# Attention scores as float32 products on two half-height tiles of TensorE, in a bucketed-attention kernel with a two-layer network behind it

## The chip, the cores and the metric

The kernel runs as one program on one core of a Trainium2 chip. What is compared is the device time of one execution in microseconds (us). The kernel before took 938.75 us, the median of three runs (938.37 to 939.9).

## The reference

```python
def _attn_ref(q, k, v, proj):                 # q, k, v: (4, 8, 768, 64) float32; proj: (64, 6)
    scale = 1.0 / np.sqrt(D)
    q_bits = (np.einsum('bhsd,dk->bhsk', q, proj) > 0).astype(np.int64)
    k_bits = (np.einsum('bhsd,dk->bhsk', k, proj) > 0).astype(np.int64)
    q_bucket = np.sum(q_bits * 2 ** np.arange(6), axis=-1)
    k_bucket = np.sum(k_bits * 2 ** np.arange(6), axis=-1)
    mask = q_bucket[:, :, :, None] == k_bucket[:, :, None, :]
    scores = np.where(mask, scale * np.matmul(q, k.transpose(0, 1, 3, 2)), -1000000000.0)
    attn = np.exp(scores - np.max(scores, axis=-1, keepdims=True))
    attn = attn / (np.sum(attn, axis=-1, keepdims=True) + 1e-09)
    return np.matmul(attn, v).astype(np.float32)

x = np.ascontiguousarray(attn_out.transpose(0, 2, 1, 3)).reshape(B * S, H * D)   # (3072, 512)
h = np.maximum(x @ w_in, 0.0)                 # w_in: (512, 2048), float64 in memory
return (h * h @ w_out).astype(np.float32)     # w_out: (2048, 512), float64 in memory
```

A query sees only the keys whose six sign bits are the same as its own. All results are wanted to nearly the precision of float32, so the kernel works with float32 products or with numbers split into a leading and a remaining part.

## The kernel before, in words

Work comes in **units** of 128 queries of one head: 4 batches x 8 heads x 6 = 192 units. `unit` (line 569) issues a unit's scores on TensorE (`pS`, 128 queries x two halves of 384 keys), the row maximum on VectorE (`nmx`), the exponential with its sum on ScalarE (`e`), the reciprocal of the sum (`rv`), the weights as a leading and a remaining float16 part (`hl`, ScalarE and VectorE) and a transposing DMA to `aT`, which brings the keys to the partitions.

`prep` (line 495) makes a head's operands. The kernel has two ways for the scores:

- The first 8 heads that are visited (`PLAIN`, line 47) are **plain**: one 128-row stack holds 64 rows of q and 64 rows of bucket indicators for one operand, k and its indicators for the other, in float32. A unit is then two float32 products of 384 columns. The profile shows each float32 product as two records, one for each of its two passes over the columns.
- The other 24 heads use the type float32r, in which a product is one pass. k and q are split into a leading and a remaining part, stacked in 128 rows as `A` and `Q`, `L` and `M`, and a unit is four products of 384 columns (`pS<-A,Q` twice, `pS<-L,M` twice).

The bucket's part comes from the **projections** `pd` (signs of 24 rows: both halves of k and of q), which ScalarE turns to `bits`, and from two products `pc` of `bits` with a table of signs, which VectorE writes into the stacks. A plain head has two float32 products `pd`, another head six float32r ones.

`av` (line 601) multiplies the weights with the values `VV` for 384 queries of one head: six products on the whole array and then, with `pair` (line 594), three times two products side by side, which go to the left and the right 64 columns of the array. For the first eight heads `av_both` (line 618) lays both halves of the queries side by side in 18 such pairs. The sum `x32` is then split into `xx` by `moe`.

`moe` (line 633) is the two-layer network for 384 tokens, eight times: 16 x 12 products `pm` of 384 columns and 16 x 9 products `po` of 512 columns, all in float32r.

Nothing is issued in the order in which it is written. `Program.order` (line 206) makes a list schedule from data, buffers and rough costs (`cost`, line 169), and `emit` (line 356) issues each engine's queue in that order; so nearly every instruction has line 382 or 379 in the profile. `PACE` ties the network's products to the units' numbers, so that they fill TensorE while attention goes on. `emit` also puts products for nothing (`idle`, line 375) where the schedule leaves TensorE idle before the first `pm`.

Of the kernel before, what the change touches and what calls it, by code (L numbers as in the profile page):

```python
# [23 lines left out]
P = 128  # L24
# [44 lines left out]
class View:  # L69
    """A part of a tile that is made when the first instruction that uses it is issued."""  # L70
# [37 lines left out]
class Program:  # L108
    """Instructions as written, and the order in which the engines' queues take them: a list
    schedule over their data, buffers and rough costs. Tile adds every wait."""  # L110
# [58 lines left out]
    def cost(key, name, args, kw):  # L169
        """(queue's time, time until the result can be used)"""  # L170
        size = lambda x: int(np.prod(x.shape[1:]))
        if name == "matmuls":
            return 188, 188
# [3 lines left out]
        if key == "pe":  # L177
            t = max(107, size(args[2]) * (4 if args[2].dtype == F32 else 1) / 2.4 + 3)
            return t, t
# [15 lines left out]
    @staticmethod  # L195
    def port(key, name, args, kw):
        """Whether the instruction takes the SBUF port that VectorE and GpSimd share."""
# [8 lines left out]
    def order(self):  # L206
# [28 lines left out]
    def backward(self):  # L235
        """For each instruction how late it could start, by a schedule from the end, latest first."""
# [42 lines left out]
    def forward(self, prio, near):  # L279
# [8 lines left out]
        out, dma, dge, held = [], 0.0, 0.0, 0.0  # L288
# [11 lines left out]
        while True:  # L300
# [94 lines left out]
def lsh_attention_moe(ctx: ExitStack, tc, kq, v, proj2, w_in, w_out, consts, out):  # L395
# [36 lines left out]
    # constants: the masks' offsets and bounds, the scales, the signs' threshold; the signs of a bucket's bits,  # L432
    # for k's and q's buckets of each half; the unit matrix
    cst = sb([P, 4], F32, "cst")
    sp.dma_start(cst, consts[:, 0:4])
    pj = sb([P, 5 * NB], F32, "pj")
    sp.dma_start(pj, proj2)
    pjh = sb([P, 5 * NB], F32R, "pjh")
    pjl = sb([P, 5 * NB], F32R, "pjl")
    move(pjh, pj)  # L440
    left(pjl, pj, 1.0, pjh.bitcast(F32))
    sgn_f = sb([4 * NB, 2 * P], F32, "sgn_f", tag="xt")
    sp.dma_start(sgn_f, consts[0 : 4 * NB, 4 : 4 + 2 * P])
    sgn = sb([4 * NB, 2 * P], BF16, "sgn")
    dve.tensor_copy(sgn, sgn_f)
    unit_f = sb([P, P], F32, "unit_f", tag="xt")
# [19 lines left out]
    def split(src, hi, lo):  # L466
        # all but each number's last two bytes: four, whose first 19 bits end the float32, and the first two
# [23 lines left out]
    # ---- operands of one head: stacks of 128 rows for the products  # L491
    f32 = lambda x: x.bitcast(F32)
    xss = {}

    def prep(b, h, plain):
        r0 = pr.rank
        dt = F32 if plain else F32R
        tags = ("A", "Q") if plain and h % 2 else ("L", "M")
        R = sb([P, S], F32, tags[0] if plain else "R", 2 if plain else 1)
        M = sb([P, S], dt, tags[1], 2)  # L500
        send(R, kq[b, h])
        if plain:
            # k, all rows but its bucket's | q, its bucket's row
            Rq = sb([D, S], F32, "Rq")
            send(Rq, kq[b, h, U])
            products, stacks = ((pj, R),), ((M, R),)
        else:
            # kh kh | qh ql, and kl, all rows but its bucket's | qh, its bucket's row
            A = sb([P, S], F32R, "A", 2)
            L = sb([P, S], F32R, "L", 2)  # L510
            Q = sb([P, S], F32R, "Q", 2)
            move(A, R, cst[:, 2:3])
            left(L, R, cst[:, 2:3], f32(A))
            products, stacks = ((pjh, A), (pjl, A), (pjh, L)), ((Q, A), (M, L))
        # sides of the projections: NB rows each for k's first and second half and for q's
        pd = ps([P, 512], F32, "pd", tag="misc")[0 : 4 * NB, 0:HS]
        todo = [(p[:, (1 - half) * NB : (5 - half) * NB], x[:, half * HS : (half + 1) * HS]) for p, x in products for half in range(2)]
        for n, (p, x) in enumerate(todo):
            pe.matmul(pd, p, x, start=n == 0, stop=n == len(todo) - 1)
        bits = sb([4 * NB, HS], BF16, "bits")  # L520
        act.activation(bits, pd, AF.Sign, scale=2.0**60, bias=cst[0 : 4 * NB, 3:4])
        pr.rank = r0 + STACKS
        if not plain:
            move(Q[T], f32(A[U]), 1.0, MV)
            move(Q[U], f32(L[U]), 1.0, MV)
            move(A[U], f32(A[T]), 1.0, MV)
        for half in range(2):
            w = slice(half * HS, (half + 1) * HS)
            pc = ps([P, 512], F32, "pc", tag="misc")[:, 0:HS]
            pe.matmul(pc, sgn[:, half * P : (half + 1) * P], bits, start=True, stop=True)  # L530
            dve.tensor_scalar(M[:, w], pc, cst[:, 0:1], cst[:, 1:2], ALU.subtract, ALU.max)
        if plain:
            move(R[U], M[T], 1.0, MV)
            move(M[T], Rq, SC)
        else:
            move(L[U], f32(M[T]), 1.0, MV)
            move(M[T], f32(Q[T]), 1.0, MV)
        return stacks
# [29 lines left out]
    # ---- 128 queries: scores, softmax, and its weights with keys on the partitions  # L568
    def unit(st, half, i, aT):
        stacks = st[0]  # L570
        c0 = half * HS + i * P
# [22 lines left out]
    def pair(pA, w, x, stop):  # L594
        """The products of two chunks of keys side by side, in the array's left and right columns."""
        pr.add((pe, "matmuls", [((pA[m, 0:HS], w[:, n], x[:, n]), {"start": False, "stop": stop}) for n, m in enumerate((T, U))], {}))
# [201 lines left out]
```

## Time and profile before

| | |
|---|---|
| runs | 938.75 us median (938.37 to 939.9) |
| span of the profiled execution | 936.9 us; what the runs' median has beyond it is 1.85 us |
| TensorE (PE) busy | 918.7 us, 98% of the span, 4865 products |
| VectorE (DVE) busy | 646.1 us, 69% |
| ScalarE (ACT) busy | 758.6 us, 81% |
| first product of the network (`pm`) | 144.7 us |
| last product | ends at 931.7 us |
| granted TensorE clock | 0.999 |

The profile gives the span of one execution from its first to its last instruction; the execution's own time is that span, and the runs' times have a little around it. Records of TensorE overlap, because the next product starts while the last one drains. So the mean duration of a product in the groups is not its price. Its price is the distance from its start to the start of the next group, which the timeline gives; there, a row is a run of like instructions with its start in us, its length, and the number of records. An operation's shape is given as the part of the array that it uses (128\*128, 128\*64: 64 of its columns, 24\*128: 24 of its rows) and the columns that stream through.

### The profile page before, as it was taken

What the parts mean: (1) busy time and instruction counts of PE and PEld (TensorE: products, weight loads), DVE (VectorE), ACT (ScalarE), POOL (GpSimd) and SP (SyncE); (2) the same over time, 40 slices, a digit from 0 to 9 for tenths busy, and PEclk for the clock granted to TensorE, in tenths of its full rate; (3) what the DMA queues carried; (4) which work ended last, traced back from release to release, by engine and by line L of the source; (5) the groups of instructions that cost most, each with busy time, mean ns of one, the idle gap of its engine ahead of it and who ended that gap; (6) DMA issues with size and microseconds to landing.
All of it is one profiled execution on the core that took longest, in us unless ns stands there. A gap on an engine that the chain in (4) does not pass through costs nothing.

```text
span 936.9 us, 14136 instructions
## 1 busy us (share of the span) xinstructions
PE 918.7 (98%) x4865; PEld 699.0 (75%) x4865; DVE 646.1 (69%) x1178; ACT 758.6 (81%) x1332; POOL 74.3 (8%) x142
## 2 busy tenths in 40 slices
PE   8999899999999999999999999999999999999997
PEld 4444447888777777777787778777786888998896
DVE  6999899999888878878788777877777322211111
ACT  5999899999999999999999998978998544433433
POOL 0210121123200000100000000000100000000000
PEclk9999999999999999999999999999999999999999
DMA  8999999999999889998899989989849853633433
GB/s 246 225 225 208 205 237 270 270 280 284 223 270 227 191 185 220 219 198 196 200 222 214 199 201 195 222 181 208 189 121 218 190 146 113 174 125 113 160 122 102
DMA packets 335643, 187.16 MB, mean 200 GB/s; under 512 B 305212, under 2 KB 305364, under 8 KB 335572
## 3 DMA queue, kind: packets, MB, share of 16 engines
q1 hardware_dynamic: 335572, 186.26, 84.2%
q8 instruction: 39, 0.64, 0.3%
q14 instruction: 32, 0.26, 0.1%
HBM read 96.04 MB, written 14.68 MB: 118 GB/s over the span
## 4 chain that ended last, share of the span: by engine, by line
PE 82%; ACT 1%; DVE 0%; issue 0%; ACTq 0%; POOL 0%; POOLq 0%
PE po L382 30%; PE pm L382 28%; PE pS L382 11%; PE pA L382 5%; PE pA L379 4%; PE pd L382 3%; PE pc L382 1%; ACT g L382 0%; ACT e L382 0%; ACT hl L382 0%; DVE f L382 0%; ACT o L382 0%; DVE nmx L382 0%; PE pt L382 0%; ACT A L382 0%
## 5 line engine op out<-in xcount | busy, mean ns | idle before, releaser
L382 PE MATMUL po<-wo,g 128*128 128x512 f32 x1152 | 365.4, 406 | 0.2 <-DVE g L382 0.2
L382 PE MATMUL pm<-xx,win 128*128 128x384 f32 x1536 | 344.2, 341 | 0.3 <-DVE g L382 0.2
L382 PEld LDWEIGHTS pm<-xx,win 128*128 128x128 f32 x1536 | 273.6, 188 | 17.2 <-issue 4.7
L382 PEld LDWEIGHTS po<-wo,g 128*128 128x128 f32 x1152 | 211.8, 188 | 49.1 <-issue 14.8
L382 DVE TENSOR_REDUCE nmx<-pS 128x1 f32<-128x768 f32 x192 | 183.1, 954 | 69.4 <-PE pS L382 68.3
L382 DVE SCALAR_TENSOR_TENSOR hl<-e,rv,hl 128x768 f16<-128x768 f32 x192 | 196.4, 1025 | 17.3 <-ACT hl L382 16.6
L382 ACT ACTIVATE e<-pS,nmx 128x768 f32<-128x768 f32 x192 | 171.8, 895 | 19.9 <-DVE nmx L382 12.6
L382 ACT ACTIVATE hl<-e,rv 128x768 f16<-128x768 f32 x191 | 176.1, 927 | 8.2 <-DMA aT<-hl 4.3
L382 DVE SCALAR_TENSOR_TENSOR g<-g,g 128x384 fp32r<-128x384 f32 x116 | 64.9, 560 | 134.8 <-ACT g L382 134.0
L382 ACT ACTIVATE g<-pm 128x384 f32<-128x384 f32 x126 | 61.3, 487 | 118.2 <-PE pm L382 117.1
L382 ACT ACTIVATE g<-g 128x384 f32<-128x384 f32 (+1 forms) x236 | 122.6, 520 | 4.2 <-DVE g L382 0.3
L382 PE MATMUL pS<-A,Q 128*128 128x384 f32 x384 | 116.9, 392 | 3.1 <-ACT e L382 2.6
L382 PE MATMUL pS<-L,M 128*128 128x384 f32 x384 | 112.3, 381 | 3.4 <-ACT e L382 2.5
L382 PEld LDWEIGHTS pS<-A,Q 128*128 128x128 f32 x384 | 68.1, 188 | 25.7 <-ACT e L382 7.2
L382 POOL TENSOR_SCALAR rv<-sm 128x1 f32<-128x1 f32 x107 | 41.5, 388 | 577.3 <-ACT e L382 573.3
L382 PEld LDWEIGHTS pS<-L,M 128*128 128x128 f32 x384 | 68.7, 188 | 16.6 <-ACT e L382 5.7
L379 PE MATMUL pA<-aT,VV 128*64 128x384 f16 x576 | 67.7, 335 | 0.5 <-DMA aT<-hl 0.5
L382 PE MATMUL pA<-aT,VV 128*128 128x384 f16 x288 | 65.8, 330 | 1.1 <-DMA aT<-hl 0.9
L379 PEld LDWEIGHTS <-VV 128*64 128x64 f16 x576 | 27.2, 108 | 40.5 <-issue 34.2
L382 PEld LDWEIGHTS <-VV 128*128 128x128 f16 x288 | 23.3, 97 | 30.4 <-issue 20.6
L382 DVE TENSOR_SCALAR M<-pc,cst 128x384 fp32r<-128x384 f32 (+1 forms) x56 | 37.6, 672 | 7.3 <-PE pc L382 6.9
L382 ACT ACTIVATION_READ_ACCUMULATOR e<-pS,nmx 128x1 f32 x192 | 36.9, 192 | 0.0
(79 smaller groups left out, 663.1 us busy)
## 6 DMA issues: line engine op xcount, KB each, us to landing
wo<-wo_d SPq DMA_DIRECT2D x112, 512.0 KB, 3.9
R<-kq SPq DMA_DIRECT2D x24, 384.0 KB, 4.4
wo_d<-wo SPq DMA_DIRECT2D x16, 512.0 KB, 4.4
raw<-w_in SPq DMA_DIRECT2D x16, 511.8 KB, 5.0
raw<-w_out SPq DMA_DIRECT2D x16, 511.8 KB, 4.7
RV<-vp SPq DMA_DIRECT2D x16, 384.0 KB, 3.9
out<-o SPq DMA_DIRECT2D x24, 256.0 KB, 3.8
aT<-hl SPq DMA_TRANSPOSE x192, 4.5
```

What stands on the lines that cost most here:

```text
L379: ins = q.engine.matmul(*map(real, args), **kw).ins
L382: ins = getattr(q.engine, o.name)(*map(real, o.args), **{k: real(x) for k, x in o.kw.items()}).ins
```

## The change

All heads now take one way. `prep` loads k as `K`, with the first 384 keys in the upper 64 partitions and the other 384 in the lower 64, and q as `Q`, the same 64 rows in both halves of the partitions. The scores of a unit are two float32 products with 64 rows each: the first runs on the array's upper 64 rows, the second on its lower 64. The bucket's indicators are no longer rows of the same stack but matrices `kM` and `qM` in bfloat16, whose two products of 64 rows are added to the scores in PSUM. No leading and remaining parts of k and q are made any more. The projections are three float32 products for each head, of 32 columns each, at column positions 0, 32 and 64 of the array; three `pc` products with 32 rows each follow.

The values of two heads of a pair are multiplied side by side: 18 times two products of 64 columns for 384 queries of both heads. The sum is split into `xx` straight from PSUM, and `x32` is gone. The visits go by pairs of heads. The schedule's costs have new numbers, and a price for a change of the type that streams (`SWITCH`). Buffers: `K`, `Q`, `kM`, `qM` have four, `hl` three instead of four, `xx` twelve instead of six.

```diff
-BUFS = dict(x32=7, xx=6, hl=4, raw=2, o=3, e=3, wo=3, aT=3)
+BUFS = dict(xx=12, hl=3, raw=2, o=3, e=3, wo=3, aT=3, K=4, Q=4, kM=4, qM=4)
-PLAIN, BOTH, ALTERNATE = 8, 12, 42
+ALTERNATE = 42
-WHOLE = {0: 6}
+WHOLE = {0: 3}
+SWITCH = 95
...
     def cost(key, name, args, kw):
         size = lambda x: int(np.prod(x.shape[1:]))
+        column = {F32: 4 / 2.4, F32R: 0.445}
         if name == "matmuls":
-            return 188, 188
+            t = max(size(a[2]) * column.get(a[2].dtype, 1 / 2.4) + 8 for a, _ in args)
+            return t, t
...
+            if k == "pe":
+                last, kind = kind, self.moving(o)
+                if last != kind:
+                    busy, done = busy + SWITCH, done + SWITCH
...
+    def matmuls(*args, start=True, stop=True):
+        pr.add((pe, "matmuls", [(a, {"start": start, "stop": stop}) for a in args], {}))
+    def prep(b, h):
         r0 = pr.rank
...
+        K = sb([P, HS], F32, "K")
+        Q = sb([P, S], F32, "Q")
+        send(K[T], kq[b, h, T, 0:HS])
+        send(K[U], kq[b, h, T, HS:])
+        send(Q[T], kq[b, h, U])
+        send(Q[U], kq[b, h, U])
+        pr.add(*[(q, "tensor_scalar", (K, K, SC, 1.0, ALU.mult, ALU.mult), {}) for q in (pool, dve)])
+        pd = ps([P, 512], F32, "pd", tag="misc")[:, 0:HS]
+        matmuls((pd[0:32], pj, K), (pd[32:64], pj, Q[:, 0:HS]), (pd[64:96], pj, Q[:, HS:]))
+        bits = sb([96, HS], BF16, "bits")
+        act.activation(bits, pd[0:96], AF.Sign, scale=2.0**60, bias=thr)
...
+        kM = sb([P, HS], BF16, "kM")
+        qM = sb([P, S], BF16, "qM")
+        for n in range(3):
             pc = ps([P, 512], F32, "pc", tag="misc")[:, 0:HS]
+            pe.matmul(pc, sgn[32 * n : 32 * n + 32], bits[32 * n : 32 * n + 32], start=True, stop=True)
+            if n == 0:
+                dve.tensor_scalar(kM, pc, NB / 2 * BIG, -BIG, ALU.subtract, ALU.max)
+            else:
+                dve.tensor_scalar(qM[:, (n - 1) * HS : n * HS], pc, NB / 2 - 1, 0.0, ALU.subtract, ALU.max)
+        return K, Q, kM, qM
...
     def unit(st, half, i, aT):
-        for s, (a, bb) in enumerate(stacks):
-            for j in range(2):
-                pe.matmul(pS[:, j, 0:HS], a[:, c0 : c0 + P], bb[:, j * HS : (j + 1) * HS], start=s == 0, stop=s == len(stacks) - 1)
+        for x, k in ((Q, K), (qM, kM)):
+            matmuls(*[(pS[:, j, 0:HS], x[m, w], k[m]) for j, m in enumerate((T, U))], start=x is Q, stop=x is qM)
...
+    def av(b, hp, half, VV, aTs):
+        pA = ps([P, 512], F32, "pA")[:, 0:HS]
+        todo = [(kc, t * D, kc + l * KC) for t, l in ((0, 0), (1, 0), (0, 1)) for kc in range(KC)]
+        for n, (kc, d0, c) in enumerate(todo):
+            matmuls(*[(pA[m], VV[:, h, kc, d0 : d0 + D], aTs[h][:, c]) for h, m in enumerate((T, U))], start=n == 0, stop=n == len(todo) - 1)
+        xx = xxs[b, half, hp] = sb([P, 2, HS], F32R, "xx")
+        move(xx[:, 0], pA, xss[b, hp])
+        left(xx[:, 1], pA, xss[b, hp], xx[:, 0].bitcast(F32))
...
-            x32, xs = x32s.pop((b, half, cc)), xss[b, cc]
-            xx = sb([P, 2, HS], F32R, "xx", BUFS["xx"])
-            move(xx[:, 0], x32, xs)
-            left(xx[:, 1], x32, xs, xx[:, 0].bitcast(F32))
-            X.append(xx)
+        X = [xxs.pop((b, half, cc)) for cc in range(NCC)]
```

Since the schedule is made anew, the order of each queue is another. The first place is a unit's scores amid the network's products on TensorE. Before, it reads like this (a row is an instruction with the tile that it writes, those that it reads, and how many of the kind follow each other):

```order
L382 MATMUL po<-wo,g 128x512
L382 MATMUL pm<-xx,win 128x384 x7
L382 MATMUL pS<-A,Q 128x384 x2
L382 MATMUL pS<-L,M 128x384 x2
L382 MATMUL pm<-xx,win 128x384 x5
```

And now, where a row `pS<-K,Q x2` is the two float32 products of a unit, upper rows first, and `qM`, `kM` are the bucket's matrices:

```order
L397 MATMUL pm<-xx,win 128x384 x12
L397 MATMUL po<-wo,g 128x512
L394 MATMUL pS<-K,Q 128x384 x2
L394 LDWEIGHTS qM
L394 MATMUL pS<-kM,qM 128x384
L394 LDWEIGHTS qM
L394 MATMUL pS<-kM,qM 128x384
L397 MATMUL po<-wo,g 128x512
```

The four float32r products, which have the network's shape, have become two float32 and two bfloat16 products of half height between products of full height.

The second place is a head's projections on TensorE. Before:

```order
L382 MATMUL po<-wo,g 128x512 x9
L382 MATMUL pd<-A,pjh 24x384 x2
L382 MATMUL pd<-A,pjl 24x384 x2
L382 MATMUL pd<-L,pjh 24x384
L382 MATMUL pS<-A,Q 128x384 x2
L382 MATMUL pS<-L,M 128x384 x2
L382 MATMUL pm<-xx,win 128x384 x2
L382 MATMUL pd<-L,pjh 24x384
```

And now:

```order
L397 MATMUL po<-wo,g 128x512 x2
L394 MATMUL pd<-K,pj 32x384
L394 MATMUL pd<-Q,pj 32x384 x2
L394 MATMUL pS<-K,Q 128x384 x2
L394 LDWEIGHTS qM
L394 MATMUL pS<-kM,qM 128x384
```

Six float32r products have become three float32 products of 32 columns, here with a unit's scores right behind them.

In all, TensorE's queue has 94 products of plain scores ahead of its first `pm` before and 98 now, 289 `idle` products before and 467 now. Counting how often a product uses another part of the array than the one ahead of it (full, 64 columns, 32 columns, 64 rows, up to 32 rows; a float32r product of 24 columns counts as full), the queue changes shape 70 times ahead of the first `pm` and 258 times behind it before, and 159 and 522 times now.

More of the change, by code (lines that the diff above doesn't have):

```diff
@@ L287, in forward @@
         free = dict.fromkeys(keys, 0.0)
-        out, dma, dge, held = [], 0.0, 0.0, 0.0
+        out, dma, dge, held, kind = [], 0.0, 0.0, 0.0, None
         def offer(i):
@@ L430, in dr @@
         return pr.tile(drp, "dram", shape, dtype, name, bufs, tag)
[L434 to L444, printed above, removed]
+    pj = sb([P, NB + 32], F32, "pj")
+    dve.memset(pj[:, 5 * NB :], 0.0)
+    sp.dma_start(pj[:, 0 : 5 * NB], proj2)
+    pj = pj[:, NB:]
+    sgn_f = sb([96, P], F32, "sgn_f", tag="o")
+    dve.memset(sgn_f, 0.0)
+    sp.dma_start(sgn_f[0:NB, T], consts[0:NB, 4 : 4 + D])
+    sp.dma_start(sgn_f[2 * NB : 3 * NB, U], consts[NB : 2 * NB, 4 + P : 4 + P + D])
+    for r0 in (32, 64):
+        for w in (T, U):
+            sp.dma_start(sgn_f[r0 : r0 + NB, w], consts[2 * NB : 3 * NB, 4 + D : 4 + P])
+    sgn = sb([96, P], BF16, "sgn")
     dve.tensor_copy(sgn, sgn_f)
-    unit_f = sb([P, P], F32, "unit_f", tag="xt")
+    thr = sb([96, 1], F32, "thr")
+    dve.memset(thr, -(2.0**-80))
+    unit_f = sb([P, P], F32, "unit_f", tag="o")
     sp.dma_start(unit_f, consts[:, 4 + 2 * P :])
@@ L489, in load_wout @@
             send(wo.bitcast(F32), wo_d[n % NF])
-    f32 = lambda x: x.bitcast(F32)
     xss = {}
-    def prep(b, h, plain):
+    def matmuls(*args, start=True, stop=True):
+        pr.add((pe, "matmuls", [(a, {"start": start, "stop": stop}) for a in args], {}))
+    def prep(b, h):
         r0 = pr.rank
[L497 to L521, printed above, removed]
-        pr.rank = r0 + STACKS
[L523 to L528, printed above, removed]
-            pc = ps([P, 512], F32, "pc", tag="misc")[:, 0:HS]
[L530 to L538, printed above, removed]
@@ L569, in unit @@
     def unit(st, half, i, aT):
-        stacks = st[0]
-        c0 = half * HS + i * P
+        K, Q, kM, qM = st
+        w = slice(half * HS + i * P, half * HS + (i + 1) * P)
         u = pr.rank
@@ L618, in av_both @@
-    def av_both(b, h, st, aTs):
-        VV = st[1][:, h % 2]
-        pA = ps([P, 512], F32, "pA")
-        hp, me = h // 2, U if h % 2 else T
-        todo = [(VV[:, kc, t * D : (t + 1) * D], kc + l * KC) for t, l in ((0, 0), (1, 0), (0, 1)) for kc in range(KC)]
-        for n, (w, c) in enumerate(todo):
-            pr.add((pe, "matmuls", [((pA[m, 0:HS], w, aT[:, c]), {"start": n == 0, "stop": n == len(todo) - 1}) for m, aT in zip((T, U), aTs)], {}))
-        for half, m in enumerate((T, U)):
-            key = (b, half, hp)
-            if key not in x32s:
-                x32s[key] = sb([P, HS], F32, "x32", BUFS["x32"])
-            move(x32s[key][me], pA[m, 0:HS])
@@ L711, in lsh_attention_moe, with ready @@
     for b in range(B):
-        F = WHOLE.get(b, H)
-        visits += [(b, h, (0, 1)) for h in range(F)] + [(b, h, (0,)) for h in range(F, H)] + [(b, h, (1,)) for h in reversed(range(F, H))]
-    u = 0
-    firsts = []
-    for vv in visits:
-        firsts.append(u)
-        u += 3 * len(vv[2])
-    stages = 0
-    pr.rank = -10.0
-    st = prep(*visits[0][:2], PLAIN > 0), values(0, 0)
+        F = WHOLE.get(b, H // 2)
+        visits += [(b, hp, half) for hp in range(F) for half in range(2)] + [(b, hp, 0) for hp in range(F, H // 2)] + [(b, hp, 1) for hp in reversed(range(F, H // 2))]
+    kept, kept_v = {}, {}
+    alive = lambda views: all(x.rec in x.rec.line[-x.rec.bufs :] for x in views)
+    def ready(b, hp, rank):
+        for h in (2 * hp, 2 * hp + 1):
+            if (b, h) not in kept or not alive(kept[b, h]):
+                pr.rank = rank
+                kept[b, h] = prep(b, h)
+        if (b, hp) not in kept_v or not alive([kept_v[b, hp]]):
+            pr.rank = rank
+            kept_v[b, hp] = values(b, hp)
+    ready(*visits[0][:2], -10.0)
     for c in range(FIRST):
@@ L727, in lsh_attention_moe @@
         load_wout(f)
-    done, kept, kept_v = {}, {(0, 0): st[0]}, {(0, 0): st[1]}
-    alive = lambda views: all(x.rec in x.rec.line[-x.rec.bufs :] for x in views)
-    for n, (b, h, halves) in enumerate(visits):
-        u, aTs, both = firsts[n], [], n < BOTH and len(halves) == 2
-        for half in halves:
+    done, u, stages = {}, 0, 0
+    for n, (b, hp, half) in enumerate(visits):
+        sts, VV, aTs = [kept[b, h] for h in (2 * hp, 2 * hp + 1)], kept_v[b, hp], []
+        for h, st in enumerate(sts):
             aT = sb([P, 2 * KC, HS], F16, "aT", BUFS["aT"])
+            aTs.append(aT)
             for i in range(3):
```

61 lines of the change are left out of this document (14 added, 47 removed).

## The prediction

> **What bounds the kernel now.** The first view is busy time by stretches, cut at the first product of the network (144.7 us) and at the end of the last one.
>
> ```profile
> core 0: us, PE busy (x) PEld busy (x) DVE busy (x) ACT busy (x) POOL busy (x), PEclk, DMA share, GB/s
> 0.00:144.70 144.70, 133.04 (x782) 68.12 (x783) 125.91 (x230) 127.45 (x217) 21.57 (x54) 1.00 1.03 226
> 144.70:931.70 787.00, 785.63 (x4085) 630.85 (x4083) 520.23 (x949) 629.63 (x1113) 52.70 (x88) 1.00 0.82 195
> ```
>
> Behind 144.7 us TensorE (PE) is busy for 785.63 of 787 us. Overlapping records can hide gaps, so the second view is what PE waited for in that stretch:
>
> ```profile
> PE pS L382 <- ACT e L382: 0.7, 1, 0.7
> PE po L382 <- DVE g L382: 0.2, 1, 0.2
> PE pm L382 <- DVE g L382: 0.2, 1, 0.2
> ```
>
> That is 1.1 us in all. VectorE works 520 us there and ScalarE 630, both with room. So behind the first `pm` the time is the sum of what PE is given, and an edit counts by the PE time that it adds or takes. What the change takes from ScalarE and VectorE (the splitting and copying of k and q, the sum `x32`) I cost at nothing there: PE's queue covers it, and the cover would be gone only if PE's sum fell by the 157 us that ScalarE has to spare. To build the sum I count PE's products in this stretch:
>
> ```profile
> L382 PE MATMUL po<-wo,g 128*128 128x512 f32 x1152 | 365.4, 406 | 0.2 <-DVE g L382 0.2
> L382 PE MATMUL pm<-xx,win 128*128 128x384 f32 x1536 | 344.2, 341 | 0.3 <-DVE g L382 0.2
> L382 PE MATMUL pS<-A,Q 128*128 128x384 f32 x288 | 79.5, 352 | 0.1
> L382 PE MATMUL pS<-L,M 128*128 128x384 f32 x294 | 77.8, 341 | 0.7 <-ACT e L382 0.7
> L382 PE MATMUL pA<-aT,VV 128*128 128x384 f16 x276 | 63.5, 330 | 0.0
> L379 PE MATMUL pA<-aT,VV 128*64 128x384 f16 x348 | 44.7, 338 | 0.0
> L382 PE MATMUL pc<-bits,sgn 24*128 24x384 bf16 x46 | 15.2, 331 | 0.0
> L382 PE MATMUL pd<-A,pjl 128*24 128x384 f32 x44 | 12.6, 338 | 0.0
> L382 PE MATMUL pd<-L,pjh 128*24 128x384 f32 x46 | 12.4, 337 | 0.0
> L382 PE MATMUL pd<-A,pjh 128*24 128x384 f32 x44 | 12.2, 350 | 0.0
> ```
>
> Prices come from distances between starts. Two runs of like products in the chain of waits give the pace of float32r:
>
> ```profile
> 200.24 2.09 PE po L382 x9
> 394.15 2.09 PE pm L382 x12
> ```
>
> 2.09/9 = 0.232 us for 512 columns (I take 0.231), 2.09/12 = 0.174 for 384. The timeline of PE gives the rest:
>
> ```profile
> 236.87 1.09 PE L382 MATMUL po<-wo,g 128*128 128x512 f32 x4
> 237.89 1.82 PE L379 MATMUL pA<-aT,VV 128*64 128x384 f16 x20
> 239.64 0.61 PE L382 MATMUL pS<-A,Q 128*128 128x384 f32 x2
> 240.09 0.51 PE L382 MATMUL pS<-L,M 128*128 128x384 f32 x2
> 240.53 1.49 PE L379 MATMUL pA<-aT,VV 128*64 128x384 f16 x16
> 241.95 0.72 PE L382 MATMUL po<-wo,g 128*128 128x512 f32 x2
> 242.52 0.52 PE L382 MATMUL pd<-A,pjh 128*24 128x384 f32 x2
> 242.87 0.34 PE L382 MATMUL pd<-A,pjl 128*24 128x384 f32 x1
> ```
>
> Here **changing the array's shape** has a price. Four `po` need 0.92 but take 1.02 (236.87 to 237.89): +0.10 ahead of the 64-column pairs. The two runs of pairs, 1.75 us for 10 and 1.42 for 8, differ by 0.33 for two pairs: about 0.16 each, which leaves 0.14 more for leaving the shape. Behind it, two float32r products of 128 columns take 0.45 (239.64 to 240.09) where 0.35 is their pace: +0.10, their first weights weren't loaded ahead. A float32r `pd` of 24 columns costs no change (242.52 to 242.87 is 0.35 for two). I book 0.20 for a change whose first product loads 128 columns of float32 weights and 0.115 for any other. In the early stage, float32 with its two passes reads:
>
> ```profile
> 62.92 1.17 PE L379 MATMUL pA<-aT,VV 128*64 128x384 f16 x12
> 64.02 0.33 PE L382 MATMUL pc<-bits,sgn 24*128 24x384 bf16 x1
> 64.28 1.56 PE L382 MATMUL pS<-A,Q 128*128 128x384 f32 x4
> 65.77 0.33 PE L382 MATMUL pc<-bits,sgn 24*128 24x384 bf16 x1
> ```
>
> `pc` takes 0.26 with its change, so 0.162 and 0.10. The four passes take 1.49; less the two halves of changes (0.10 of late weights, 0.10 ahead of `pc`) that is 0.322 a pass.
>
> **Does the sum hold for the kernel before?** `pm` 267.3, `po` 266.1, scores 576 x 0.174 + 6 passes x 0.322 = 102.1, `pA` 276 x 0.162 + 174 pairs x 0.160 = 72.5, `pd` 134 x 0.174 = 23.3, `pc` 46 x 0.162 = 7.5, 258 changes (119 onto 128 columns of float32, 139 others) 23.9 + 16.0 = 39.9, small ones 0.6: 779.3 us, against 787.0 measured, 1% short. PE's own sum explains this stage.
>
> **The change behind the first `pm`, part by part.** Counts are from the new queue.
>
> - *Network*: the same 533.4 us.
> - *Scores*: 143 units. Float32 score pairs on half-height tiles don't occur before, so this is the unknown. Each product has two passes, and the queue holds upper first, upper second, lower first, lower second. The lower tile's first pass can run beside the upper's second, if each start keeps the queue's order; then the pair takes 3 x 0.322 = 0.966. Bounds: 0.644, the two products wholly side by side, like the float16 pairs at 0.160 for two; 1.288, one after the other, like the four passes above. I take 0.966, since passes of one product follow each other in every row, and nothing before shows a start that overtakes. The bucket's pair is 0.162: its upper half can start beside the last lower pass. 143 x (0.966 + 0.162) = 161.3, for 102.1: **+59.2**.
> - *Projections*: 21 heads, three products of two passes each, in a chain by the same reasoning: 4 x 0.322 = 1.288 (0.644 to 1.932). 27.0 for 23.3: **+3.7**.
> - *Buckets*: 66 `pc` x 0.162 = 10.7 for 7.5: **+3.2**.
> - *Values*: 450 pairs x 0.160 = 72.0 for 72.5: **-0.5**.
> - *Changes of shape*: 522, of which 360 onto 128 columns of float32: 72.4 + 18.6 = 91.0 for 39.9: **+51.1**. A unit's scores had the network's shape; now each unit leaves it and comes back. That half-height tiles of 128 columns cost what the other shapes cost is an estimate from the rows above; from nothing to 0.20 for the 305 changes that touch them, it is 0 to 57.6 us of the 91.
>
> Together 779.3 becomes 896.0: **+116.7 us**.
>
> On the order of starts: the Trainium skill (TensorE: Matmul & The Clock Gate, Part 3, "What overlaps and what doesn't") says that products start and end strictly in program order, and that only weight loads are pulled ahead. By that rule the pair is 0.966 and the time is the forecast's. No run so far shows it for two float32 tiles.
>
> **The early stage** is bound by several engines at once:
>
> ```profile
> 14.00:126.00 112.00, 105.02 (x567) 51.15 (x567) 102.95 (x185) 103.84 (x178) 17.67 (x43) 1.00 1.04 215
> ```
>
> Of 112 us PE is busy for 105, DVE for 103, ACT for 104. Relief for ACT alone buys nothing. PE's work changes by: scores 49 x 1.128 - 47 x 1.288 = -5.2; projections +2.1, `pc` +1.9, values 0, changes of shape 159 for 70: +12.5. That is +11 us; 178 more `idle` products would be +10 if nothing covers them. Below, nothing, since PE has some slack here; above, 21. I take +11, as most of the fillers stand where the schedule expects PE to wait. SP gets about 88 more loads (four a head), at 0.3 us each by this row:
>
> ```profile
> 12.08 0.33 SPq L382 DMA_DIRECT2D raw<-w_in  x1
> ```
>
> A transposing DMA may stand behind one for 0.3 us; the units in flight cover that, and if they didn't it would be 0.3 x 88 = 26 us at the very most.
>
> **Sum.** 936.9 + 116.7 + 11 = 1064.6 us of span. The runs' median lies 1.85 us over the span before, so 1066 us. This forecast's own range is 1030 (half-height changes at 0.115, no early loss) to 1095 (more fillers, weights that are late at each tile).
>
> **Rivals.**
>
> *A, wholly side by side* (0.644 a pair). For it: float16 pairs cost as much as one. Against: there each product has one pass, and nothing stands between the two starts. Behind the first `pm` it saves 143 x 0.322 + 21 x 0.644 = 59.6, leaving +57.1; early PE drops below DVE, which holds the stage at 0. 936.9 + 57.1 + 1.85 = 996 us. The Trainium skill (TensorEngine Tiling (Array Packing), "Theoretical Speedup") promises up to 2x for contractions of 64, which would be this rival's time.
>
> *B, one after the other* (1.288, bucket's pair 0.324, projections 1.932). For it: no half-height pair of any type is in the trace. Against: the 64-column pairs do overlap. +82.7 behind the first `pm`, +31 early: 1180 us.
>
> *C, not slower*: the two tiles act as arrays of their own, each taking its next pass when its own rows are free, so that a unit neither drains the array nor waits for the other tile. Then A's saving comes with all 305 changes at nothing: 116.7 - 59.6 - 57.6 = -0.5, early 0 or a few us less: 930 to 939 us. For it: the float32r `pd` of 24 columns changes shape freely. Against: `pc` pays, and so does a float32 `pd` of 24 columns, as the 1.40 us here for four passes of 0.322 show:
>
> ```profile
> 14.95 1.47 PE L382 MATMUL pd<-A,pj 128*24 128x384 f32 x4 [0.31 <-DVE big L382]
> 16.35 0.91 PE L382 MATMUL pS<-L,M 128*128 128x384 f32 x2
> ```
>
> It decides only once pair and changes together fall by 117 us, 0.8 us for each unit.
>
> **How the numbers follow.** Forecast 0.60, A 0.21, B 0.12, C 0.07 (half of it and a bit faster, the rest within 0.2%, which is about what the runs' scatter of this kernel can tell from no change). So faster 0.04, same 0.03, slower 0.93. The likeliest gives 1066 us. The range takes in A and the dear end of the forecast, and leaves out B and C: 975 to 1125.
>
> **What would show it.** Score passes 0.32 us apart with three steps a unit (right), two steps (A) or four (B). About 0.1 us more than the pace on the product ahead of a unit's scores, and again on the one behind them. PE still waiting for next to nothing behind the first `pm`, and that `pm` at 145 to 165 us. ScalarE and VectorE with shorter busy time and longer idle time, without gain. The forecast is wrong in kind if PE has gaps behind the first `pm`, since then the sum no longer is the time, or if a unit's scores and both changes take under 0.8 us.

## The result, and the profile after

The changed kernel takes 1022.24 us (median of three runs, 1016.55 to 1023.71), against 938.75 us before: 1.087 times as long, with an interval of 1.0827 to 1.0914. Its profiled execution has a span of 1020.3 us, 83.4 us more than before.

The busy times by stretches, cut again at the first product of the network (`pm`, now at 156.8 us) and at the end of the last product:

```profile
core 0: us, PE busy (x) PEld busy (x) DVE busy (x) ACT busy (x) POOL busy (x), PEclk, DMA share, GB/s
0.00:156.80 156.80, 133.38 (x1114) 67.75 (x1114) 127.73 (x240) 108.45 (x189) 22.28 (x61) 0.95 0.97 202
156.80:1015.50 858.70, 844.31 (x4651) 586.59 (x4649) 483.22 (x939) 515.78 (x945) 29.10 (x47) 1.00 0.76 186
```

The 83.4 us lie in two places: the early stage is 12.1 us longer, the stretch behind it 71.7 us (858.7 for 787.0). In that stretch PE is busy for 58.7 us more (844.3 for 785.6) and without work for 13.0 us more (14.4 for 1.4). ScalarE lost 114 us of work and VectorE 37, and neither helped.

The groups of PE in that stretch have the counts of the prediction (286 scores of two passes each, 66 `pc`, 450 pairs):

```profile
L394 PE MATMUL pS<-K,Q 64*128 64x384 f32 x572 | 131.7, 537 | 10.5 <-ACT e L397 10.4
L394 PE MATMUL pA<-aT,VV 128*64 128x384 f16 x900 | 85.8, 329 | 0.0
L394 PE MATMUL pS<-kM,qM 64*128 64x384 bf16 x288 | 47.6, 324 | 0.0
L397 PE MATMUL pc<-bits,sgn 32*128 32x384 bf16 x66 | 22.1, 335 | 3.8 <-ACT bits L397 2.2 <-DVE qM L397 1.5
```

New is what stands behind the second bar: PE waited 10.4 us for ScalarE's exponential before a unit's scores, and 3.8 us before a `pc`. At the end of one wait the granted clock (the last but two of the figures) falls to half for 6.8 us:

```profile
731.40:738.20 6.80, 6.37 (x19) 4.14 (x18) 4.48 (x8) 3.61 (x7) 0.00 (x0) 0.50 0.89 196
```

PE's 6.37 us there are about 3.2 us of work at full clock, so 3.2 of the 844.3 us are the clock's. What a unit costs shows in PE's timeline:

```profile
505.00 1.20 PE L397 MATMUL po<-wo,g 128*128 128x512 f32 x4
506.12 0.92 PE L394 MATMUL pS<-K,Q 64*128 64x384 f32 x4
506.87 0.33 PE L394 MATMUL pS<-kM,qM 64*128 64x384 bf16 x2
507.13 0.73 PE L397 MATMUL po<-wo,g 128*128 128x512 f32 x2
507.80 0.33 PE L397 MATMUL pc<-bits,sgn 32*128 32x384 bf16 x1
```

The four passes of a unit's scores take 0.75 us (506.12 to 506.87). Less the 0.10 of late weights that is 0.645, two steps of 0.322: the two products run side by side in all their passes. In the records behind this row the upper and the lower tile's first passes start 7 ns apart, the second ones 0.42 us later and again 7 ns apart. It is no chance unit: 133 of the 143 in the stretch take 0.75 us from the first pass to the bucket's product. The bucket's pair takes 0.26 = 0.16 + 0.10 for leaving the shape, and two `po` behind it take 0.67 where 0.46 is their pace, of which 0.10 is late weights and 0.10 the next change, to `pc`. So the shapes' prices are those that were read before. A unit that stands alone among the network's products takes 0.81 us of products and 0.40 us of changes, 1.21 us, where four float32r products took 0.70.

The projections run side by side too:

```profile
402.85 0.51 PE L394 MATMUL pd<-K,pj 128*32 128x384 f32 x1
402.86 0.52 PE L394 MATMUL pd<-Q,pj 128*32 128x384 f32 x2
403.20 0.49 PE L394 MATMUL pd<-K,pj 128*32 128x384 f32 x1
403.20 0.49 PE L394 MATMUL pd<-Q,pj 128*32 128x384 f32 x2
403.63 1.20 PE L397 MATMUL po<-wo,g 128*128 128x512 f32 x4
```

Two groups of three passes, 0.78 us in all with the change behind them.

With 0.644 for the score pairs and the projections in place of 0.966 and 1.288, the prediction's sum for this stretch is 896.0 - 59.6 = 836.4 us, 57.1 over before. The scores are then 143 x 0.806 = 115.3 for 102.1, the projections 13.5 for 23.3, `pc` 10.7 for 7.5, and the changes of shape 91.0 for 39.9. So 51 of the 57 us are changes of shape. PE's busy time rose by 58.7, of which 3.2 are the half clock.

### The profile page after: what moved, and what is told of

It reads as the page before. It is cut to its first block, busy times and chain, and to the rows that moved or that the text cites. A ratio compares the mean times of both kernels' runs of the same rounds, so it can differ in the third digit from the quotient of the medians.

```text
span 1020.3 us, 15765 instructions
## 1 busy us (share of the span) xinstructions
PE 977.7 (96%) x5763; PEld 654.3 (64%) x5763; DVE 611.0 (60%) x1178; ACT 625.8 (61%) x1135; POOL 51.4 (5%) x108
## 4 chain that ended last, share of the span: by engine, by line
PE 60%; DMA 4%; DVE 1%; ACT 1%; issue 1%; SPq 0%; ACTq 0%; DVEq 0%
PE pm L397 23%; PE po L397 21%; PE pS L394 9%; PE pA L394 5%; DMA aT<-hl 3%; PE pc L397 1%; PE pd L394 1%; DMA K<-kq 1%; DVE nmx L397 1%; DVE hl L397 1%; ACT e L397 0%; ACT hl L397 0%; SPq L397 0%; ACT o L397 0%; DVE VV L397 0%
## 5 line engine op out<-in xcount | busy, mean ns | idle before, releaser
L397 PE MATMUL po<-wo,g 128*128 128x512 f32 x1152 | 343.0, 406 | 0.0
L394 PE MATMUL pS<-K,Q 64*128 64x384 f32 x768 | 179.6, 543 | 24.8 <-ACT e L397 24.0
L394 PE MATMUL pA<-aT,VV 128*64 128x384 f16 x1152 | 114.2, 335 | 3.0 <-DMA aT<-hl 3.0
L394 PEld LDWEIGHTS pS<-K,Q 64*128 64x128 f32 x768 | 58.7, 186 | 83.5 <-ACT e L397 44.2
L394 PEld LDWEIGHTS <-VV 128*64 128x64 f16 x1152 | 61.0, 111 | 58.9 <-issue 35.7
L394 PE MATMUL pS<-kM,qM 64*128 64x384 bf16 x384 | 63.9, 328 | 0.0
L390 PEld LDWEIGHTS <-ones 128*128 128x128 bf16 x467 | 28.3, 102 | 20.2 <-issue 19.0
L397 PE MATMUL pc<-bits,sgn 32*128 32x384 bf16 x96 | 32.3, 337 | 7.7 <-ACT bits L397 4.2
L397 DVE TENSOR_SCALAR qM<-pc 128x384 bf16<-128x384 f32 x64 | 35.1, 548 | 7.5 <-PE pc L397 7.3
L390 PE MATMUL idle<-ones 128*128 128x128 bf16 x467 | 36.3, 228 | 1.2 <-DVE ones L397 1.2
```

The lines of the kernel that those rows point to most:

```text
L390: issue(q, q.engine.matmul(self.idle[0].real(), self.idle[1].real(), self.idle[1].real(), start=True, stop=True).ins)
L394: ins = q.engine.matmul(*map(real, args), **kw).ins
L397: ins = getattr(q.engine, o.name)(*map(real, o.args), **{k: real(x) for k, x in o.kw.items()}).ins
```

## The experiments

All times are of the whole kernel. "Stretch" is the time from the first product of the network to the end of the last product, "gaps" is the stretch less PE's busy time in it. The theory to begin with: PE's work is the time, and changes of shape are most of the added work. The rival: the loss is waiting, and the changes are hidden.

### Does each half of the array keep its own order?

In `emit`, the lower scores were held back until the upper bucket's product had been issued:

```diff
-                for args, kw in o.args:
+                todo = o.args
+                if len(todo) == 2 and todo[0][0][0].rec in held or len(todo) == 2 and todo[0][0][2].dtype == F32:
+                    rec = todo[0][0][0].rec
+                    if rec not in held:
+                        held[rec] = todo[1]
+                        todo = todo[:1]
+                    else:
+                        todo = [todo[0], held.pop(rec), todo[1]]
+                for args, kw in todo:
```

> The changed kernel with a unit's four products in another order: upper scores, upper bucket, lower scores, lower bucket, in place of upper scores, lower scores, upper bucket, lower bucket. In the changed kernel's trace the passes of the two scores alternate (upper first and lower first start 7 ns apart, then the two second passes). Theory 1 (each start follows the queue, and the two scores' passes are interleaved only because they stand next to each other): the lower scores start beside the upper bucket, a unit takes 0.32 + 0.32 + 0.32 + 0.32 + 0.16 = 1.45 us in place of 0.81, +92 us behind the first product of the network and 10 to 30 early: 1120 to 1145 us. Theory 2 (each half of the array takes its own next pass when it is free): no change, 1016 to 1028 us.

Measured: 1025.57 us (one run), stretch 861.8. The kernel's PE timeline:

```profile
500.37 0.92 PE L402 MATMUL pS<-K,Q 64*128 64x384 f32 x4
501.12 0.33 PE L402 MATMUL pS<-kM,qM 64*128 64x384 bf16 x2
501.38 0.74 PE L405 MATMUL po<-wo,g 128*128 128x512 f32 x2
```

It is 0.75 and 0.26 again. The queue now has upper scores and upper bucket ahead of the lower scores, and still the lower scores' first pass starts 10 ns behind the upper one's, ahead of two things that stand before it in the queue. It is the same in all 134 units whose four products stand together. So the order of starts does not hold between the halves of the array; within a half nothing here breaks it. The prediction's reason for 0.966 is refuted, by a case that it would have priced at 1.45 us a unit. The Trainium skill (TensorE: Matmul & The Clock Gate, Part 3, "What overlaps and what doesn't") has products strictly in program order; for row tiles this run, with its 10 ns, does not agree.

### The price of one more change of shape

Behind each unit's float32 scores a product for nothing was put, whose result goes to columns of PSUM that are not read:

```diff
+                    issue(q, q.engine.matmul(pS[:, 0, HS:512], self.idle[1].real(), self.idle[1].real(), start=False, stop=False).ins)
```

(`self.idle[1]` is the matrix `ones`.) So a unit leaves its shape and comes back once more, two changes.

> The changed kernel with one product more in each unit, for nothing, on the full 128x128 array (128 columns of bfloat16, 0.056 us), put between the unit's float32 scores and its bucket's products; the rest of the order is as it was. Theory 1 (changes of shape cost PE time): each unit leaves the half-height shape once more, 0.056 + 2 x 0.115 = 0.29 us, times 143 units behind the first product of the network = +41 us, and up to +14 early: 1062 to 1078 us. Theory 2 (the loss is PE waiting for other engines; changes are mostly hidden): only the product's own 0.056 x 192 = +8 to +11 us: 1030 to 1034 us.

The control does the same work in the shape that the unit has:

```diff
+                    issue(q, q.engine.matmul(pS[:, 0, HS:512], one[0:D], one[0:D], start=False, stop=False).ins)
+                    issue(q, q.engine.matmul(pS[:, 1, HS:512], one[D:P], one[D:P], start=False, stop=False).ins)
```

> The control for the run before: the same place, but the product for nothing is done as two half-height products of 64 rows side by side (0.056 us for both), in the shape that the unit has anyway. Both theories: +8 us behind the first product of the network, up to +3 early: 1028 to 1034 us. If this costs about as much as the full-height product, the price is for any product more, not for the shape.

Measured: 1043.82 us with the full product, 1020.36 us with the two halves (one run each). The first kernel's PE timeline, and its busy time behind the first product of the network:

```profile
501.53 0.92 PE L394 MATMUL pS<-K,Q 64*128 64x384 f32 x4
502.38 0.23 PE L398 MATMUL pS<-ones 128*128 128x128 bf16 x1
502.54 0.34 PE L394 MATMUL pS<-kM,qM 64*128 64x384 bf16 x2
502.81 0.73 PE L400 MATMUL po<-wo,g 128*128 128x512 f32 x2
```

```profile
156.90:1037.00 880.10, 877.24 (x4794) 597.69 (x4792) 485.47 (x938) 517.35 (x944) 28.60 (x47) 1.00 0.75 181
```

and the control's:

```profile
500.71 0.92 PE L394 MATMUL pS<-K,Q 64*128 64x384 f32 x4
501.46 0.22 PE L398 MATMUL pS<-ones 64*128 64x128 bf16 x1
501.47 0.22 PE L399 MATMUL pS<-ones 64*128 64x128 bf16 x1
501.52 0.33 PE L394 MATMUL pS<-kM,qM 64*128 64x384 bf16 x2
501.78 0.61 PE L401 MATMUL pm<-xx,win 128*128 128x384 f32 x2
```

```profile
151.10:1013.60 862.50, 852.05 (x4937) 600.67 (x4935) 483.81 (x939) 516.09 (x944) 27.55 (x47) 1.00 0.77 185
```

From the scores to the next `po` it is now 1.28 us where it was 1.01: +0.27 for a product of 0.056, against 0.29 expected. In the control it is 1.07, +0.06. So the price belongs to the change of shape. PE is busy for 32.9 us more (877.2 for 844.3), and for 36 more at full clock, since this run has no half clock in the stretch: 134 units with their four products together, at 0.27 each, are 36. The control's same work costs 7.7 us (8 expected). But the whole rose by 21.6 us, half of what theory 1 gave, and lies between the ranges of the two theories; the control lies 8 us under its range. PE's gaps fell as its work grew, from 14.4 us to 2.9 and in the control to 10.5, with the order of the queue the same but for the added products. Both theories had a part of it. The changes are PE work at the price that was read, and beside that PE waits for something that goes away when PE is later.

### Fewer changes of shape

The values' 36 products, and a unit's four, became one block each in the schedule, and `pc` got 128 rows with zeros:

```diff
-            pe.matmul(pc, sgn[32 * n : 32 * n + 32], bits[32 * n : 32 * n + 32], start=True, stop=True)
+            pe.matmul(pc, sgn3[:, n], bits, start=True, stop=True)
...
-        for x, k in ((Q, K), (qM, kM)):
-            matmuls(*[(pS[:, j, 0:HS], x[m, w], k[m]) for j, m in enumerate((T, U))], start=x is Q, stop=x is qM)
+        pr.add((pe, "matmuls", [((pS[:, j, 0:HS], x[m, w], k[m]), {"start": x is Q, "stop": x is qM})
+                                for x, k in ((Q, K), (qM, kM)) for j, m in enumerate((T, U))], {}))
...
-        for n, (kc, d0, c) in enumerate(todo):
-            matmuls(*[(pA[m], VV[:, h, kc, d0 : d0 + D], aTs[h][:, c]) for h, m in enumerate((T, U))], start=n == 0, stop=n == len(todo) - 1)
+        pr.add((pe, "matmuls", [((pA[m], VV[:, h, kc, d0 : d0 + D], aTs[h][:, c]), {"start": n == 0, "stop": n == len(todo) - 1})
+                                for n, (kc, d0, c) in enumerate(todo) for h, m in enumerate((T, U))], {}))
```

> The changed kernel with fewer changes of shape: the 36 products of the values of two heads are one block that nothing is put into, so are a unit's scores and bucket products, and the three bucket products of a head run on the full array with zeros in the other rows. By the new queue, changes behind the first product of the network fall from 522 (360 onto 128 columns of float32) to 343 (283). Theory 1 (each costs 0.115 or 0.20): 90.6 -> 63.5, and +2 us of other work: -25 us, 993 to 1003 us. Theory 2 (the loss is waiting): blocks make other work wait longer, so no gain: 1015 to 1030 us.

Measured: 1000.96 us, 1.0683 times before (1.0621 to 1.0744). PE's busy time behind the first product of the network fell to 821.4 us, by 22.9 (25 expected; 19.7 of it is work, as this run has no half clock in the stretch), and its gaps rose from 14.4 us to 20.3:

```profile
152.90:994.60 841.70, 821.39 (x4669) 589.46 (x4669) 483.50 (x936) 521.56 (x960) 24.52 (x46) 1.00 0.80 190
```

Fewer changes give the time back, as theory 1 has it.

### Full-height float32 instead

The kernel before, with all heads on the plain way:

```diff
-PLAIN, BOTH, ALTERNATE = 8, 12, 42
+PLAIN, BOTH, ALTERNATE = 32, 12, 42
```

> The kernel before with all 32 heads plain: a unit is two float32 products on the full array, four passes of 0.322 = 1.288 us, with no change of shape for scores, in place of four float32r products (0.70) for 24 heads. Theory 1 (in the changed kernel a unit pays 0.81 for its products and 0.40 for its two changes of shape, so full-height float32 costs nearly the same): 144 x 0.59 = +85 us, projections in float32 +6, with their changes of shape +6: 1025 to 1042 us, within 2% of the changed kernel. Theory 2 (half-height tiles save the whole 0.48 us of a unit over full height): it would be 60 to 70 us over the changed kernel, 1080 or more.

Measured: 1030.89 us, 1.0985 times before (1.096 to 1.1009), 1% over the changed kernel; its gaps are 9.9 us. PE's timeline of a unit:

```profile
506.40 1.45 PE L382 MATMUL pS<-L,M 128*128 128x384 f32 x4
507.69 0.22 PE L382 MATMUL pt<-dg,ones 128*128 128x128 bf16 x1
```

Four passes in 1.29 us, full height and no change on either side. So full height costs 1.29 us a unit, and half height 0.81 + 0.40 = 1.21. The half-height tiles do save 0.48 us of passes; the array's shape takes 0.40 of it.

### What PE waits for in the changed kernel

The gaps were open. One of them in the changed kernel, over all engines:

```profile
723.25 8.05 SPq L397 DMA_TRANSPOSE aT<-hl  x2
...
730.38 0.94 ACT L397 ACTIVATE hl<-e,rv 128x768 f16<-128x768 f32 x1 [3.00 <-DMA aT<-hl]
731.22 0.56 ACT L397 ACTIVATE bits<-pd,thr 96x384 bf16<-96x384 f32 x1
...
731.83 0.47 PE L397 MATMUL pc<-bits,sgn 32*128 32x384 bf16 x1 [2.22 <-ACT bits L397]
```

ScalarE waits 3.00 us at `hl` for a transposing DMA, so `bits` come late, and PE stands 2.22 us before `pc` with the network's products behind it in its queue. In this stretch ScalarE waits 22.1 us for transposing DMAs at `hl`, where it was 1.4 before. Buffers were the first suspects. (The next three runs also have the smaller buffers that their expectations name.)

```diff
-BUFS = dict(xx=12, hl=3, raw=2, o=3, e=3, wo=3, aT=3, K=4, Q=4, kM=4, qM=4)
+BUFS = dict(xx=12, hl=4, raw=2, o=2, e=3, wo=3, aT=3, K=4, Q=4, kM=4, qM=4)
```

> The changed kernel with four buffers for the weights' parts hl, as before the change, in place of three (room for it: o has two buffers in place of three, xs eight in place of twelve). In the changed kernel PE is without work for 14.3 us behind the first product of the network, mostly since a unit's scores wait for the exponential of the unit ahead, and ScalarE stands at hl until a transposing DMA has read an older buffer. Theory 1 (three buffers of hl make that wait): PE's gaps fall to 5 us or less, 1008 to 1015 us. Theory 2 (the order that the schedule makes and the single buffer of scores make it): gaps of 10 us or more stay, 1016 to 1026 us.

Measured: 1028.54 us, 1.0947 (1.0911 to 1.0984); gaps 21.0 us. Theory 1 falls; the time lies over theory 2's range too.

```diff
-BUFS = dict(xx=12, hl=3, raw=2, o=3, e=3, wo=3, aT=3, K=4, Q=4, kM=4, qM=4)
+BUFS = dict(xx=12, hl=3, raw=1, o=2, e=3, wo=3, aT=4, K=4, Q=4, kM=4, qM=4)
```

> The changed kernel with four buffers aT in place of three; room for it comes from raw (one buffer in place of two), the converted tops (one in place of two), o (two in place of three) and xs. In the changed kernel a pair of heads holds two aT until its values are multiplied, so one is left for the next transposing DMA, and PE's gaps of 14.3 us behind the first product of the network stand where hl waits for such a DMA. Theory 1 (the third aT is what the DMA waits for): gaps fall to 6 us or less, and the stretch behind the first product of the network falls by 6 to 10 us against the control with three aT. Theory 2 (order of the schedule, DMA engines that are busy): gaps stay at 10 to 20 us, the stretch changes by under 4 us.

> The control for the run before: the same smaller buffers (raw, tops, o, xs) with three aT as in the changed kernel. Both theories: gaps of 10 to 20 us as in the changed kernel, 1018 to 1032 us.

Measured: 1035.55 us with four `aT` (1.1017, 1.0994 to 1.104), 1033.2 with three (1.1006, 1.0986 to 1.1027); gaps 17.7 and 14.8, stretches 872.7 and 864.1. No gain either, and the control lies 1 us over its range. The two have different orders (557 and 534 changes of shape behind the first product of the network, by their queues), so a difference of a few us says nothing.

The second suspect was the schedule's prices. First the dearer one:

```diff
-SWITCH = 95
+SWITCH = 200
```

> The changed kernel with SWITCH = 200 in place of 95, so that the schedule prices a change of the type that streams nearer to the 0.20 us that changes onto float32 weights take. Only the order can change. Theory 1 (the gaps come from an order made for prices that are too low): gaps fall to 7 us or less, 1008 to 1016 us. Theory 2 (they come from a buffer or the DMA): gaps of 10 us or more, 1016 to 1030 us.

Measured: 1057.11 us, 1.1249 (1.123 to 1.1268), beyond both ranges:

```profile
160.60:1051.50 890.90, 859.09 (x4667) 593.61 (x4667) 487.26 (x943) 522.55 (x950) 20.45 (x45) 0.99 0.75 180
```

The gaps are 31.8 us, twice as long, with about the same changes of shape (515). PE's busy time rose too, by 14.8 us; why was not followed up. That was against theory 1, and pointed the other way: the dearer the schedule takes PE to be, the more PE waits. A new theory: this queue doesn't wait where PE is late against the schedule, since then everything else is early. So prices that are too low:

```diff
-SWITCH = 95
+SWITCH = 0
...
-        column = {F32: 4 / 2.4, F32R: 0.445}
+        column = {F32: 4 / 2.4, F32R: 1 / 2.4}
```

It was run on the grouped kernel, where the number of changes stays, and on the changed kernel itself.

> The kernel after_grouped with a schedule that believes PE to be quicker than it is: SWITCH = 0 in place of 95, float32r at 1/2.4 ns a column in place of 0.445. Changes of shape behind the first product of the network stay about the same (347 for 343), so only who is late differs. Theory 1 (PE has gaps since the schedule puts other engines' results just in time, and any of them that is late stalls PE's queue; with PE late against the schedule its work is always ready): gaps fall from 20.2 us to 6 us or less, 984 to 992 us. Theory 2 (the gaps are a lack of the kernel's buffers or of DMA time): gaps of 12 us or more, 997 to 1008 us.

> The changed kernel with the same lower prices, without the blocks. Its new order has 657 changes of shape behind the first product of the network (427 onto 128 columns of float32) in place of 522 (360), which by the booked prices is +21 us of PE time. Theory 1 (late PE has no gaps): gaps fall from 14.3 us to 5 us or less, and the whole is 1022 + 21 - 10 = 1028 to 1038 us. Theory 2 (gaps from buffers or DMA): gaps stay, 1040 to 1050 us.

Measured: 989.71 us, 1.0555 (1.0534 to 1.0577), for the grouped one, and 1030.99, 1.0985 (1.0955 to 1.1015), for the other. PE in the grouped kernel:

```profile
158.00:982.90 824.90, 821.84 (x4657) 589.70 (x4657) 474.70 (x909) 516.48 (x949) 33.88 (x62) 1.00 0.79 192
```

and in the other:

```profile
161.70:1025.60 863.90, 861.84 (x4654) 584.05 (x4652) 471.09 (x901) 513.98 (x944) 39.12 (x71) 1.00 0.76 181
```

Gaps of 3.1 and 2.1 us, at the same buffers. The grouped pair is the clean case: PE's busy time is 821.4 and 821.8 (3.3 of the latter from 6.8 us of half clock at its start), and the gaps are 20.3 and 3.1. The stretch is 16.8 us shorter, the whole 11.3, since the first product of the network comes 5.1 us later. So an order alone, without another buffer, takes PE's waits away. That the cause is PE being late against the schedule is what the theory forecast; the run in which full-height products were added (gaps 2.9 us) agrees, as there PE is later in the same order. No run changed the prices of the kernel before.

### A version that beats both

The same grouping applied to the kernel before: three pairs (or 18) as one block, `pc` on the full array.

```diff
-    sgn = sb([4 * NB, 2 * P], BF16, "sgn")
-    dve.tensor_copy(sgn, sgn_f)
+    sgn = sb([P, 2 * P], BF16, "sgn")
+    dve.memset(sgn, 0.0)
+    dve.tensor_copy(sgn[0 : 4 * NB], sgn_f)
+    bits = sb([P, HS], BF16, "bits")
+    dve.memset(bits, 0.0)
...
-        for kc in range(0, KC, 2):
-            pair(pA, VV[:, kc : kc + 2, 0:D], aT[:, KC + kc : KC + kc + 2], kc == KC - 2)
+        pr.add((pe, "matmuls", [((pA[m, 0:HS], VV[:, kc + n, 0:D], aT[:, KC + kc + n]), {"start": False, "stop": kc == KC - 2})
+                                for kc in range(0, KC, 2) for n, m in enumerate((T, U))], {}))
...
```

> The kernel before with fewer changes of shape and nothing else: the three 64-column pairs of a head (18 where both halves go side by side) are one block, and the bucket products pc run on the full array, with zeros in the rows above 24. By the new queue, changes behind the first product of the network fall from 258 (119 onto 128 columns of float32) to 96 (42). Theory 1 (each costs 0.115 or 0.20): 39.8 -> 14.6, other work +1 us: -24 us, 912 to 920 us. Theory 2 (changes are cheap where PE has other work in its queue, or the blocks make PE wait as much): 932 to 942 us.

Measured: 925.11 us, 0.9843 times before (0.982 to 0.9866).

```profile
148.90:919.00 770.10, 766.17 (x4087) 629.74 (x4087) 515.71 (x938) 625.55 (x1110) 66.46 (x96) 1.00 0.82 197
```

PE is busy for 19.5 us less behind the first product of the network (24 expected), waits 2.6 us more, and that product comes 4.2 us later. So 12.7 us of the span remain, 13.6 between the medians. The time lies between the ranges of the two theories, but PE's own time fell by most of what theory 1 has.

## Why the prediction was right, and where it was wrong

The direction was right, and the time lies in the stated range of 975 to 1125 us. But 1022 us is under the forecast's own range (1030 to 1095), between the forecast's 1066 and rival A's 996. It is as near as it is in part by luck, since waits that the sum did not have gave back 13 of the 60 us by which it was too dear. The parts:

- **PE's sum is the time behind the first `pm`**: right for 98% of the stretch. With the true price of a pair the sum gives 836.4 us; PE was busy for 844.3, about 1% more, as it was for the 779.3 and 785.6 before, and 3.2 us of it are half clock. But the prediction had named gaps behind that product as the sign that it would be wrong in kind, and 14.4 us of them came.
- **Changes of shape, +51.1**: right. The prices at half-height tiles (0.10 ahead, 0.10 behind, 0.10 of late weights) are those that the other shapes showed, and two changes that were added cost 0.27 us with their product for 0.29. (By the prediction's own counts and prices the term is 90.6, not 91.0: 360 x 0.20 is 72.0.)
- **Scores, +59.2, and projections, +3.7**: wrong. The step that failed is "if each start keeps the queue's order; then the pair takes 3 x 0.322 = 0.966". It takes 0.644, also where the queue's order speaks against it: scores +13, projections -10. Rival A had this price. That was 59.6 us too much.
- **"PE's queue covers it"**: wrong in part. PE's gaps rose from 1.4 to 14.4 us, which no step of the sum had. The runs on the changed kernel suggest why: before, PE would have been so late against its schedule that all else was ready, and the new prices in the schedule are nearer to the truth. On the kernel before this was not tried.
- **Early stage, +11**: 12.1 measured, which is luck, as the reason given does not hold. With pairs at 0.644 PE's work there would fall, not rise. (The count of 70 changes of shape before also left out 18 around float32 `pd` of 24 columns, which pay by the prediction's own row. With 88, its +12.5 would be about +10, an estimate.) PE's busy time is 133.4 us for 133.0, part of it at half clock (0.95 on average for 1.00), and it is without work for 23.4 us where it was 11.7. What makes it wait more was not tried, but most of the difference is in the wait for ScalarE's exponential (us in all, times, longest), before and now:

```profile
PE pS L382 <- ACT e L382: 4.4, 11, 0.8
```

```profile
PE pS L394 <- ACT e L397: 13.7, 12, 4.1
```

- **Values, -0.5**: the pairs' pace is as it was. ScalarE's and VectorE's relief bought nothing, as expected.

So the forecast's 44 us of error are 59.6 of passes that were too dear, less 13.0 of gaps, 1.6 of PE's busy time (the half clock is more than that) and 1.1 in the early stage. Rival A, whose mechanism is the true one, misses by 26: the early stage (+12), the gaps (+13) and 1.6 of busy time. Rival B and rival C are refuted by the same rows: the halves overlap, and each change of shape is paid. C's idea that each half takes its next pass when its rows are free was right; that the changes would cost nothing was not.

## What to carry to other kernels

Where TensorE is the bound, count how often its queue changes the array's shape and multiply: here 0.10 us on each side and 0.10 more when 128 columns of float32 weights come next, which ate 0.40 of the 0.48 us that a half-height pair saved over full height. Keep narrow products together or give them full height with zeros; the two together took about 1.5% off the kernel before. And when a list schedule's prices for the bounding engine are corrected, look at that engine's gaps: in the changed kernel, prices that are too low kept its queue from waiting.

## What the runs showed of the hardware

Two products on the upper and the lower half of the array run side by side pass by pass, 7 to 10 ns apart, and a product on one half starts ahead of products for the other half that stand before it in the queue. A change of shape costs about 0.1 us each time whether it is by rows or by columns, in float32 and in 16-bit types, and also from one partial shape to another: from a unit's first pass to the next start it is 1.01 us whether the network (95 units), 64-column pairs (23), `pd` (6) or `pc` (8) follows. Float32r products of 24 columns are the one narrow kind here that paid nothing. In the changed kernel a wait of 2.22 us (before 731.83) came with 6.8 us of half clock, while waits of 1.67 us (before 208.53) and 1.45 us (before 442.90) did not.
